# Attention, two mixtures of experts: another order for the last expert, narrower passes for two others

## The chip, the cores and the metric

One core of one Trainium2 chip runs the whole program. The metric is the device time of one execution in microseconds (us). Engines are named as in the profile: PE is TensorE (PEld its weight loads), ACT is ScalarE, DVE is VectorE, POOL is GpSimd, SP is SyncE, which issues most transfers.

## The reference

Three stages follow each other. The change touches the second and its seam to the third.

```python
# 1: attention over 4 x 8 heads, window 32 and 32 global tokens; x is [2176, 512]
# 2: top-1 mixture of 8 experts
logits = x @ w_gate
e_idx = np.argmax(logits, axis=1)
...
for e in range(E):                        # E = 8
    mask = e_idx == e
    h = np.maximum(x[mask] @ w1[e], 0.0)  # 512 -> 1024
    ye = h @ w2[e]                        # 1024 -> 512
    out[mask] = gate_w[mask, None] * eom[mask, e, None] * ye
# 3: the last stage, 512 -> 2048 -> 512, with a rational function between
h = x @ w_in
P = a[0] + a[1] * h + a[2] * h2 + a[3] * h3
Q = 1.0 + np.abs(b[0]) * np.abs(h) + np.abs(b[1]) * h2
g = P / (Q + 1e-06)
return g @ w_out
```

The inputs of the measurement send 422, 331, 253, 249, 220, 149, 434 and 118 tokens to the experts 0 to 7.

## The kernel before, in words

**Numbers.** Each float32 operand of these products is split into a rounded part (`fp32r`, "hi") and the rest ("lo"); a product is made of hi x hi, hi x lo and lo x hi. ScalarE makes the hi part with a cast, and VectorE or GpSimd the lo part with a subtraction. Weights come in 16 pieces of 128 x 512 an expert (`split_piece`); pieces 0 to 7 are w1, 8 to 15 are w2. There are two weight buffers, `slot[0]` and `slot[1]`, in turn, and four raw buffers, so that a raw load waits until the pieces two loads back are split.

**A wide pass** (`wide`, lines 918 to 960) holds weights in TensorE and streams an expert's tokens: in each of 8 steps 12 matmuls make 128 rows of h for n tokens (line 932), ScalarE and VectorE make ReLU with hi and lo (937, 938), and two steps later 12 matmuls add to four accumulators (944). That is 192 matmuls of n columns. `WIDE` gives n for some experts, `BASE` = 256 for the others. At the end four copies (950) bring the result to `yt`, and two DMAs on ScalarE's queue store it (952, 869).

**A single block** (`single`, 875 to 916) does it the other way round: 128 tokens lie in TensorE, and the weights stream past them, 512 columns a matmul. 24 matmuls make h with tokens in rows (895), a ReLU (898), 8 transposes (883) with casts and subtractions (809, 810) turn it, then products by w2 (905), two copies that make `y` (910 by ScalarE, 911 by VectorE), four transposes (914), a copy (915) and a store. With `parts=2` the second products have 256 columns and use two accumulators, with `parts=1` 512 and one. `beyond(e)` runs it behind a branch when an expert has more tokens than its pass; here that happens for expert 0 and for expert 6. It stands behind the first step of the next expert's pass.

**Side work.** While TensorE works through a pass, `todo` gives the other engines work at fixed points, *ticks*: `wide` takes one tick after every six matmuls. `plan` says what is done at which tick: "s" splits a weight piece of the next expert, "c" does one of three operations that convert a piece of w_in or w_out from its 64-bit form (`conv_step`, VectorE; 18 pieces, three at each of experts 1 to 6, with a load and a store by SP), "g" gathers 128 tokens, "x" scales and "p" transposes and splits them. In expert 7's pass (`PLANW7`) the pieces split are those of w_in for the last stage (`MODE7`: how), and `first_steps` is woven in: it splits the first 512 rows of stage 3's input into `x2c` (`x2_prep`, 1189 and 1190), and does the first two of the last stage's 16 groups: per group 12 matmuls in two halves ("m"), and in five parts ("e") the rational function: three activations, a GpSimd product and two VectorE operations; Ln and Exp; three VectorE operations; the rounding (1182); the subtraction (1184).

**The seam.** Behind expert 7 come `beyond(7)`, a first spare product of the last stage (group 2), the split of two W_out pieces (`first_w`, 1117 and 1118), a branch for rare inputs (1126) and a second spare product (group 3, both line 1150). Then the last stage runs in steps of 12 + 12 matmuls (1150 and 1295). All engines take their instructions in the order in which the program gives them.

Of the kernel before, what the change touches and what calls it, by code (L numbers as in the profile page):

```python
# [7 lines left out]
F32 = mybir.dt.float32  # L8
# [34 lines left out]
READY, WIDE = (6,), {0: 296, 1: 332, 6: 308}  # L43
# [13 lines left out]
NPRE, NCONV = 2, 9  # L57
# [3 lines left out]
PLANW = plan(32, s=range(0, 31, 2), c=(2, 3, 4, 12, 13, 14, 22, 23, 24), g=(1, 3, 18, 24), x=(1, 2, 14, 16), p=(5, 8, 19, 22))  # L61
PLANW7 = plan(30, s=(0, 5, 6, 8, 9, 11, 12, 14, 15, 17, 18, 20, 21, 23, 24, 25))
# [38 lines left out]
MODE7 = ("act",) + ("act_pool",) * 15  # L101


class Build:
# [731 lines left out]
    def experts(self, st, first, gate):  # L836
# [38 lines left out]
        def single(e, to, x, at=0, put=None, parts=2):  # L875
# [16 lines left out]
            for n in range(2):  # L892
                ph = ps_a.tile([128, 512], F32, tag=f"acc{n + 1}", name=f"acc{n + 1}")
                for i, (k, a, b) in enumerate(ORDER):
                    nc.tensor.matmul(ph, lhsT=x[:, a, k, at:at + 128], rhs=W[:, b, 2 * k + n, :], start=(i == 0), stop=(i == 11))
                    if i % 3 == 2:
                        hook(n, i // 3)
                nc.scalar.activation(hr[n], ph, AF.Relu)
            w = 512 // parts
            py = [ps_a.tile([128, 512], F32, tag=f"acc{m}", name=f"acc{m}")[:, 0:w] for m in (0, 3)[:parts]]  # L900
            for ks in [(k,) for k in range(6)] + [(6, 7)]:
# [5 lines left out]
                for k in ks:  # L907
                    hook(2, k)
            y, yc = hr[0], hr[1].rearrange("p (c t) -> p c t", c=4)
# [52 lines left out]
        def todo(e, plan, half=None, blocks=(), gathers=(), mode=SPLIT_MODE):  # L962
# [3 lines left out]
            k = NCONV * (e - 1)  # L966
# [26 lines left out]
        blocks = lambda e, bs=range(4): [(e, b, b) for b in bs if e < E]  # L993

# [29 lines left out]
        def expert(e, early=lambda: ()):  # L1024

            plan = PLANW if e < E - 1 else PLANW7
            more_ = blocks(e + 1, (2, 3)) if e + 1 in READY else [None] * 2
            wide(e, wd(e), X(e), weave(todo(e, plan, None, blocks(e + 1, (0, 1)) + more_, more_ + blocks(e + 2, (0, 1))),
# [65 lines left out]
        def first_steps(at=None):  # L1094

            def tick(n):
                while at and at[0] < n:
                    at[0] += 1
                    yield
            for n in range(CH[0]):  # L1100
                yield from tick(1 + n)
                self.x2_prep(n, self.x2c, n)
            h = [ps_t().tile([128, 4, 128], F32, tag="pt", name="pt").rearrange("p c t -> p (c t)") for _ in range(2)]
            gens = [self.first_elem(k, h[k], hr[k]) for k in range(2)]
            order = [("m", 0), ("m", 0), ("e", 0), ("m", 1), ("m", 1), ("e", 0), ("e", 1), ("e", 0), ("e", 1), ("e", 1)]
            parts = [self.product_parts(h[k], self.x2c, k, 512) for k in range(2)]
            for i, (c, k) in enumerate(order):
                yield from tick(8 + i + i // 2)
                next(parts[k] if c == "m" else gens[k], None)
            for k, t in enumerate(GT + (30, 30)):  # L1110
# [8 lines left out]

        expert(E - 2, early)  # L1120
        expert(E - 1, lambda: first_steps([0]))
# [348 lines left out]
```

## Time and profile before

| | us |
|---|---|
| median of 3 runs | 778.82 (778.63 to 778.91) |
| the profiled execution | 779.69 |
| its span, first to last instruction | 778.0 |
| busy in the span: PE / PEld | 757.1 / 652.5 |
| busy in the span: DVE / ACT / POOL | 584.4 / 527.3 / 352.7 |
| mean granted TensorE clock | 0.993 |

The profiled execution is one of its own, 0.11% above the median; stretches are read from its trace and set against its own time. A busy PE is not a PE at its peak, since matmuls overlap: for what a matmul costs, the distance from one start to the next is read.

### The profile page before, as it was taken

How to read it: one execution, taken by the hardware profiler on the slowest of the kernel's cores; microseconds unless marked ns; L12 is line 12 of the kernel's file. 1: busy time of each engine (PE TensorE's matmuls, PEld its weight loads, DVE VectorE, ACT ScalarE, POOL GpSimd, SP SyncE). 2: the span in 40 equal slices, each digit the busy share in tenths (PEclk: the TensorE clock that was granted, in tenths of full speed). 3: DMA queues.
4: the chain of work that ended last, by engine and by line, in shares of the span. 5: the costliest groups of instructions: out<-in, count | busy, mean ns of one | idle time of the engine just before them, and what ended most of it. 6: DMA issues, size and time to landing. Idle time of an engine off the chain costs nothing. (4 is left out here: it accounts for less than half of the span.)

```text
span 778.0 us, 16683 instructions
## 1 busy us (share of the span) xinstructions
PE 757.1 (97%) x5976; PEld 652.5 (84%) x5976; DVE 584.4 (75%) x1419; ACT 527.3 (68%) x1181; POOL 352.7 (45%) x439
## 2 busy tenths in 40 slices
PE   8998999899999999999999999999999999999996
PEld 5776776698999999998978888898888898989984
DVE  5777788683568877772389998888888768997983
ACT  4666775555455656643778887778777767887872
POOL 4445664523255556541756866532342214322422
PEclk9999999999999999999999999999999999999998
DMA  8998885555588999893463340110010000000101
GB/s 290 323 312 273 291 269 144 144 168 184 191 279 285 316 304 334 287 306 114 127 195 109 109 108 1 51 45 14 1 54 14 1 1 27 28 1 1 40 1 40
DMA packets 51978, 112.55 MB, mean 145 GB/s; under 512 B 10194, under 2 KB 24274, under 8 KB 49832
## 3 DMA queue, kind: packets, MB, share of 16 engines
q1 hardware_dynamic: 42232, 96.39, 39.1%
q0 software_dynamic: 3168, 9.27, 3.4%
q10 hardware_dynamic: 6480, 5.65, 2.3%
q8 instruction: 52, 0.85, 0.5%
q14 instruction: 46, 0.38, 0.2%
HBM read 93.58 MB, written 18.77 MB: 144 GB/s over the span
## 5 line engine op out<-in xcount | busy, mean ns | idle before, releaser
L1256 POOL TENSOR_TENSOR q<-q,ab 128x384 f32<-128x384 f32 (+1 forms) x78 | 93.9, 1204 | 212.1 <-ACT q L1255 205.1
L1295 PE MATMUL acc<-slot,gh 128*128 128x512 f32 x528 | 165.7, 394 | 0.0
L699 POOL TENSOR_TENSOR slot<-raw,slot 128x512 fp32r<-128x512 f32 x66 | 90.3, 1377 | 89.0 <-ACT slot L695 86.9
L1150 PE MATMUL ph<-x2c,slot 128*128 128x512 f32 (+1 forms) x552 | 125.1, 374 | 0.9 <-DVEq L1126 0.6
L1150 PEld LDWEIGHTS ph<-x2c,slot 128*128 128x128 f32 x552 | 101.1, 187 | 19.6 <-DVEq L1126 0.9
L1295 PEld LDWEIGHTS acc<-slot,gh 128*128 128x128 f32 x528 | 98.3, 187 | 20.1 <-ACT gh L1267 0.2
L944 PE MATMUL acc<-hT,slot 128*128 128x256 f32 (+3 forms) x768 | 109.2, 292 | 0.0
L1295 PE MATMUL acc<-slot,gl 128*128 128x512 f32 x264 | 104.4, 395 | 0.0
L944 PEld LDWEIGHTS acc<-hT,slot 128*128 128x128 f32 x768 | 101.9, 189 | 0.2
L695 ACT CAST slot<-raw 128x512 fp32r<-128x512 f32 x128 | 75.0, 618 | 7.6 <-DVE yt L950 4.0
L316 POOL TENSOR_SCALAR pr<-ex,r 128x128 f32<-128x128 f32 x128 | 47.0, 379 | 60.8 <-PE sc L263 21.0
L1150 PE MATMUL ph<-xa,slot 128*128 128x384 f32 x384 | 71.8, 336 | 0.0
L1150 PEld LDWEIGHTS ph<-xa,slot 128*128 128x128 f32 x384 | 67.9, 188 | 2.7
L1267 ACT CAST gh<-u 128x384 fp32r<-128x384 f32 (+1 forms) x78 | 43.3, 555 | 39.0 <-PE acc L1295 20.8
L699 DVE TENSOR_TENSOR slot<-raw,slot 128x512 fp32r<-128x512 f32 x62 | 55.0, 890 | 14.9 <-ACT slot L695 14.4
L1270 ACT ACTIVATE r<-q,cab 128x384 f32<-128x384 f32 (+1 forms) x78 | 51.3, 657 | 19.3 <-POOL q L1256 18.7
L937 ACT ACTIVATE hT<-ph 128x256 fp32r<-128x256 f32 (+3 forms) x64 | 25.7, 401 | 50.8 <-PE ph L932 40.1
L1295 PEld LDWEIGHTS acc<-slot,gl 128*128 128x128 f32 x264 | 49.4, 187 | 12.3 <-DVE gl L1268 0.3
L298 ACT ACTIVATE ex<-sm,mx 128x128 f32<-128x128 f32 x128 | 50.3, 395 | 13.9 <-POOL pr L316 7.0
L1255 ACT ACTIVATE q<-ab,cab 128x384 f32<-128x384 f32 (+1 forms) x78 | 58.3, 747 | 0.9
L1255 ACT ACTIVATE u<-ph,cab 128x384 f32<-128x384 f32 (+1 forms) x78 | 55.0, 705 | 4.0 <-POOL gl L1268 2.8
L932 PE MATMUL ph<-xa,slot 128*128 128x256 f32 (+1 forms) x384 | 54.6, 292 | 1.2 <-PEq L1040 0.4
(235 smaller groups left out, 1471.0 us busy)
## 6 DMA issues: line engine op xcount, KB each, us to landing
raw<-in_w_dram SPq DMA_DIRECT2D x78, 512.0 KB
vw<-in_vw_dram SPq DMA_DIRECT2D x16, 1024.0 KB
r<-in_w_dram SPq DMA_DIRECT2D x18, 512.0 KB
kw<-in_kw_dram SPq DMA_DIRECT2D x16, 384.0 KB
raw<-wf SPq DMA_DIRECT2D x9, 512.0 KB
qt<-in_qT_dram SPq DMA_DIRECT2D x32, 128.0 KB
xbuf<-xrow SPq DMA_DIRECT2D x8, 512.0 KB
xg<-ybuf SPq DMA_DIRECT2D x13, 256.0 KB
```

What stands on the lines that cost most here:

```text
L298: nc.scalar.activation(ex[:, h], src[:, h], AF.Exp, bias=mx[:, h:h + 1], scale=-1.0, accum_out=ssum[:, h:h + 1])
L316: nc.gpsimd.tensor_scalar(out=pr[:, h], in0=ex[:, h], scalar1=r[:, h:h + 1], scalar2=1.0, op0=ALU.mult, op1=ALU.mult)
L695: nc.scalar.copy(hi, r)
L699: eng.tensor_tensor(out=lo[:, c], in0=r[:, c], in1=hi[:, c].bitcast(F32), op=ALU.subtract)
L932: nc.tensor.matmul(ph, lhsT=W[:, b, 2 * k + s // 4, c:c + 128], rhs=x[:, a, k, :n], start=(i == 0), stop=(i == 11))
L944: nc.tensor.matmul(acc[m][:, :n], lhsT=W[:, b, 8 + f, 128 * m:128 * m + 128], rhs=hT(f % nh, n)[:, a], start=(f == 0 and i == 0), stop=(f ...
L1150: self.nc.tensor.matmul(ph[:, :w], lhsT=l[a], rhs=r[b], start=(k == 0 and i == 0), stop=(k == 3 and i == 2))
L1255: nc.scalar.activation(o_, x_, AF.Identity, scale=k1, bias=k0)
L1256: nc.gpsimd.tensor_tensor(out=q, in0=q, in1=ab, op=ALU.mult)
L1267: nc.scalar.copy(g[0], up)
L1270: nc.scalar.activation(r0, q, AF.Ln, bias=eps1)
L1295: nc.tensor.matmul(accs[i], lhsT=l[a], rhs=Wo[:, b, f, :], start=(f == 0 and j == 0), stop=(f == 15 and j == 2))
```

## The change

Expert 7 has no wide pass any more: behind expert 6's pass comes `beyond(6)`, then `single` for expert 7's 128 tokens with `parts=1`, and the side work and the last stage's first two groups are taken from inside it (`bg`): a tick after three matmuls of the first products, after each ReLU, and after each of the eight steps of the second, 16 in all; what is left of the side work follows behind `single`. `ORDER1` puts the parts of the two groups on ticks; their accumulators are now `acc3` and `acc1`, and a scratch tile is part of `yt`. `PLANW7` has 18 ticks, and in `MODE7` two pieces have their subtraction on VectorE instead of one. The result of expert 7 is stored by `put_last`. Experts 4 and 5 get passes of 224 and 160 columns. The 18 conversions go to the experts as `PIECES` says: 6, 3, 3, 2, 1, 3 for experts 1 to 6. Expert 7 has one block of tokens gathered and prepared, not two (`pair`).

```diff
--- before.py
+++ after.py
@@ -40,7 +40,7 @@
 NB = 2
 BASE, MOST, LAG = 256, 512, 2
 NX = 4
-READY, WIDE = (6,), {0: 296, 1: 332, 6: 308}
+READY, WIDE = (6,), {0: 296, 1: 332, 4: 224, 5: 160, 6: 308, 7: 128}
 FIRST = WIDE[0]
 SA, S0, S1 = "v", "a", "a"
 
@@ -54,12 +54,18 @@
     return o
 
 
-NPRE, NCONV = 2, 9
+NPRE = 2
+PIECES = 0, 6, 3, 3, 2, 1, 3, 0
 
 LOADS = [(f, f + 1) for f in range(0, NPRE, 2)] + [(f,) for f in range(NPRE, 16)]
 WLO = lambda nc, f: nc.vector if f < 3 else nc.gpsimd
-PLANW = plan(32, s=range(0, 31, 2), c=(2, 3, 4, 12, 13, 14, 22, 23, 24), g=(1, 3, 18, 24), x=(1, 2, 14, 16), p=(5, 8, 19, 22))
-PLANW7 = plan(30, s=(0, 5, 6, 8, 9, 11, 12, 14, 15, 17, 18, 20, 21, 23, 24, 25))
+EACH = {6: (1, 4, 8, 12, 16, 20), 3: (2, 12, 22), 2: (3, 12), 1: (12,), 0: ()}
+PLANW = lambda e: plan(32, s=range(0, 31, 2), c=[k + n for k in EACH[PIECES[e]] for n in range(3)], g=(1, 3, 18, 24), x=(1, 2, 14, 16), p=(5, 8, 19, 22))
+PLANW7 = plan(18, s=(0, 0, 5, 5, 6, 7, 9, 9, 11, 11, 12, 13, 14, 15, 16, 17))
+ORDER1 = ((4, "m", 0), (5, "m", 0), (8, "e", 0), (9, "m", 1), (11, "m", 1), (11, "e", 0), (13, "e", 1), (14, "e", 0),
+          (16, "e", 1), (17, "e", 1))
+GT1 = 18, 19
+ORDER0 = tuple((0, c, int(k)) for c, k in ("m0", "m0", "e0", "m1", "m1", "e0", "e1", "e0", "e1", "e1"))
 EY = 11, 1, 11, 1
 GT = 25, 27
 ORDER = 13
@@ -98,7 +104,7 @@
 W0 = lambda s: s >= 25
 NWARM = 12
 SPLIT_MODE = ("act_pool", "act")
-MODE7 = ("act",) + ("act_pool",) * 15
+MODE7 = ("act",) * 2 + ("act_pool",) * 14
 
 
 class Build:
@@ -872,7 +878,7 @@
 
             nc.sync.dma_start(out=self.ybuf[:, :, FIRST:FIRST + 128], in_=y)
 
-        def single(e, to, x, at=0, put=None, parts=2):
+        def single(e, to, x, at=0, put=None, parts=2, bg=iter(())):
 
             W = self.slot[e % 2]
             hk = lambda a, k: hT(AFTER + k // 2, BASE)[:, a, 128 * (k % 2):128 * (k % 2) + 128]
@@ -895,7 +901,10 @@
                     nc.tensor.matmul(ph, lhsT=x[:, a, k, at:at + 128], rhs=W[:, b, 2 * k + n, :], start=(i == 0), stop=(i == 11))
                     if i % 3 == 2:
                         hook(n, i // 3)
+                        if i < 11:
+                            next(bg, None)
                 nc.scalar.activation(hr[n], ph, AF.Relu)
+                next(bg, None)
             w = 512 // parts
             py = [ps_a.tile([128, 512], F32, tag=f"acc{m}", name=f"acc{m}")[:, 0:w] for m in (0, 3)[:parts]]
             for ks in [(k,) for k in range(6)] + [(6, 7)]:
@@ -906,6 +915,7 @@
                                              start=(k == 0 and i == 0), stop=(k == 7 and i == 2))
                 for k in ks:
                     hook(2, k)
+                    next(bg, None)
             y, yc = hr[0], hr[1].rearrange("p (c t) -> p c t", c=4)
             nc.scalar.copy(y[:, :256], py[0][:, 0:256])
             nc.vector.tensor_copy(y[:, 256:], py[-1][:, w - 256:w])
@@ -963,7 +973,7 @@
 
 
             sp = self.split_set(e + 1, mode if e < E - 1 else MODE7, half)
-            k = NCONV * (e - 1)
+            k = 3 * sum(PIECES[:e])
             gs, xs, ps, ns = iter(gathers), iter(blocks), iter(blocks), self.counts()
             for do in plan:
                 for c in do:
@@ -992,6 +1002,8 @@
 
         blocks = lambda e, bs=range(4): [(e, b, b) for b in bs if e < E]
 
+        pair = lambda e: blocks(e, range(min(2, -(-wd(e) // 128)))) + [None] * (wd(e) <= 128)
+
         def fetch(e, i):
 
             ixo = self.ixo[:, 0:1]
@@ -1023,9 +1035,9 @@
 
         def expert(e, early=lambda: ()):
 
-            plan = PLANW if e < E - 1 else PLANW7
+            plan = PLANW(e) if e < E - 1 else PLANW7
             more_ = blocks(e + 1, (2, 3)) if e + 1 in READY else [None] * 2
-            wide(e, wd(e), X(e), weave(todo(e, plan, None, blocks(e + 1, (0, 1)) + more_, more_ + blocks(e + 2, (0, 1))),
+            wide(e, wd(e), X(e), weave(todo(e, plan, None, pair(e + 1) + more_, more_ + pair(e + 2)),
                                          iter(early())), before=(lambda: beyond(e - 1)) if e > 1 else second)
 
         def beyond(e):
@@ -1093,21 +1105,28 @@
 
         def first_steps(at=None):
 
+            order, late = (ORDER1, GT1) if at else (ORDER0, (0, 0))
+
             def tick(n):
                 while at and at[0] < n:
                     at[0] += 1
                     yield
             for n in range(CH[0]):
-                yield from tick(1 + n)
+                yield from tick(n)
                 self.x2_prep(n, self.x2c, n)
-            h = [ps_t().tile([128, 4, 128], F32, tag="pt", name="pt").rearrange("p c t -> p (c t)") for _ in range(2)]
-            gens = [self.first_elem(k, h[k], hr[k]) for k in range(2)]
-            order = [("m", 0), ("m", 0), ("e", 0), ("m", 1), ("m", 1), ("e", 0), ("e", 1), ("e", 0), ("e", 1), ("e", 1)]
-            parts = [self.product_parts(h[k], self.x2c, k, 512) for k in range(2)]
-            for i, (c, k) in enumerate(order):
-                yield from tick(8 + i + i // 2)
-                next(parts[k] if c == "m" else gens[k], None)
-            for k, t in enumerate(GT + (30, 30)):
+            h, parts, gens = {}, {}, {}
+            for t, c, k in order:
+                yield from tick(t)
+                if c == "m":
+                    if k not in h:
+                        acc = f"acc{3 - 2 * k}"
+                        h[k] = ps_a.tile([128, 512], F32, tag=acc, name=acc)
+                        parts[k] = self.product_parts(h[k], self.x2c, k, 512)
+                        gens[k] = self.first_elem(k, h[k], yt.rearrange("p m t -> p (m t)")[:, 512 * k:512 * k + 512])
+                    next(parts[k], None)
+                else:
+                    next(gens[k], None)
+            for k, t in enumerate(late + late):
                 yield from tick(t)
                 next(gens[k % 2], None)
 
@@ -1117,8 +1136,18 @@
                 nc.scalar.copy(hi, w)
                 nc.vector.tensor_tensor(out=lo, in0=w, in1=hi.bitcast(F32), op=ALU.subtract)
 
+        def put_last(y):
+            k = 128 - NBLK * (E - 1)
+            YQ(nc).dma_start(out=self.toks[bass.ds(off[E - 1], 128 * k), :].rearrange("(j p) o -> j (p o)", p=128),
+                             in_=self.idxT[NBLK * (E - 1):])
+            store(E - 1, 0, 128, y, YQ(nc))
+
         expert(E - 2, early)
-        expert(E - 1, lambda: first_steps([0]))
+        beyond(E - 2)
+        side = weave(todo(E - 1, PLANW7), first_steps([0]))
+        single(E - 1, 0, X(E - 1), parts=1, bg=side, put=lambda y: put_last(y))
+        for _ in side:
+            pass
         beyond(E - 1)
         self.bank = [ps_h.tile([128, 512], F32, tag="ph", name="ph") for _ in range(PRE)]
         first_w()
```

## Rows read from the trace of the kernel before

**Rows 1.** Windows, experts 1, 5, 7: PE, PEld, DVE, ACT, POOL busy; clock, DMA, GB/s.

```profile
184.00:226.00 42.00, 40.95 (x268) 39.20 (x269) 21.03 (x31) 17.69 (x36) 12.96 (x11) 1.00 0.61 198
298.30:323.45 25.15, 25.00 (x211) 24.83 (x210) 20.25 (x32) 16.68 (x35) 16.83 (x12) 1.00 0.96 330
367.20:394.70 27.50, 27.40 (x204) 26.08 (x204) 13.02 (x24) 21.27 (x42) 20.86 (x17) 1.00 0.39 126
```

**Rows 2.** Timeline of TensorE, 350 to 404 us: start, us, what [idle before <-releaser].

```profile
351.98 1.60 PE L932 MATMUL ph<-xa,slot 128*128 128x256 f32 x12
353.42 4.25 PE L895 MATMUL acc<-slot,x2c 128*128 128x512 f32 x18
357.51 0.60 PE L883 MATMUL pt<-ident,hr 128*128 128x128 f32 x4
357.86 1.65 PE L895 MATMUL acc<-slot,x2c 128*128 128x512 f32 x6
...
367.24 3.14 PE L932 MATMUL ph<-xa,slot 128*128 128x256 f32 x24 [0.43 <-PEq L1040]
...
394.79 3.64 PE L1150 MATMUL ph<-x2c,slot 128*128 128x512 f32 x13
399.03 2.83 PE L1150 MATMUL ph<-x2c,slot 128*128 128x512 f32 x11 [0.59 <-DVEq L1126]
401.70 2.68 PE L1295 MATMUL acc<-slot,xa 128*128 128x512 f32 x11
```

**Rows 3.** Timeline of ScalarE, 358 to 398 us.

```profile
358.14 0.37 ACT L809 CAST hT<-pt 128x256 fp32r<-128x256 f32 x1 [1.20 <-PE pt L883]
359.01 0.37 ACT L809 CAST hT<-pt 128x256 fp32r<-128x256 f32 x1 [0.49 <-DVE hT L810]
...
367.82 0.62 ACT L695 CAST slot<-raw 128x512 fp32r<-128x512 f32 x1 [0.34 <-ACTq L1040]
...
377.58 0.60 ACT L1166 ACTIVATE hr<-pt 128x512 f32<-128x512 f32 x1 [2.30 <-issue]
...
379.44 0.38 ACT L937 ACTIVATE hT<-ph 128x256 fp32r<-128x256 f32 x1
379.71 1.66 ACT L695 CAST slot<-raw 128x512 fp32r<-128x512 f32 x3
...
394.51 0.31 ACTq L952 DMA_DIRECT2D toks<-idxT  x1
...
396.27 1.14 ACT L1117 CAST slot<-raw 128x512 fp32r<-128x512 f32 x2 [1.58 <-ACTq L1037]
```

**Rows 4.** Timeline of VectorE, 386 to 391 us.

```profile
388.11 0.68 DVE L1176 SCALAR_TENSOR_TENSOR xg<-xg,pt 128x512 f32<-128x512 f32 x1
```

**Rows 5.** Weight loads by shape, whole span: busy us, mean ns | idle before.

```profile
L944 PEld LDWEIGHTS acc<-hT,slot 128*128 128x128 f32 x768 | 101.9, 189 | 0.2
...
L883 PEld LDWEIGHTS pt<-ident,hr 128*128 128x128 f32 x16 | 1.9, 140 | 0.3
...
L339 PEld LDWEIGHTS pt<-ident,exg 128*32 128x32 f32 x8 | 0.8, 98 | 0.0
```

**Rows 6.** Windows around the one fall of the clock behind the start.

```profile
135.70:139.13 3.43, 2.29 (x33) 1.32 (x29) 2.08 (x11) 2.03 (x7) 3.36 (x7) 1.00 0.62 158
139.13:142.54 3.41, 3.36 (x30) 2.32 (x34) 2.01 (x9) 1.86 (x7) 2.99 (x6) 0.50 0.01 2
```

**Rows 7.** Timeline of TensorE in the passes of experts 4 and 5.

```profile
291.31 1.59 PE L944 MATMUL acc<-hT,slot 128*128 128x256 f32 x12
292.74 1.54 PE L932 MATMUL ph<-x2c,slot 128*128 128x256 f32 x12
294.12 1.10 PE L944 MATMUL acc<-hT,slot 128*128 128x256 f32 x8
...
311.16 1.60 PE L932 MATMUL ph<-xa,slot 128*128 128x256 f32 x12
312.59 0.64 PE L944 MATMUL acc<-hT,slot 128*128 128x256 f32 x4
```

## The prediction

> **What bounds the kernel now.** I read the windows first, one per stage. In the pass of expert 5 TensorE is busy 25.00 of 25.15 us, ScalarE 16.68, VectorE 20.25; in the rest of expert 7's pass TensorE is busy 27.40 of 27.50, ScalarE 21.27, GpSimd 20.86 [rows 1]. So TensorE sets the time of both stretches, but in the second the other engines are not far behind. Then the timeline of TensorE from expert 6's last product to the third product of the last stage, to see where it waits: 0.43 us behind the single block of expert 6, and 0.59 us ahead of the second spare product, released by VectorE passing a branch [rows 2]. Then the timelines of ScalarE and VectorE in the same stretch, for the price and the order of what has to fit beside TensorE [rows 3, 4]. Last, weight loads by shape and a fall of the clock [rows 5, 6].
>
> **Expert 4 at 224 and expert 5 at 160 columns.** Each pass keeps its 192 matmuls; only the columns shrink. Today 12 matmuls of 256 columns take 1.38 us in expert 4's first product (292.74 to 294.12) and 1.43 in its second (291.31 to 292.74), 1.43 in expert 5 (311.16 to 312.59) [rows 7]: 115, 119 and 119 ns each. If time went with columns, 224 would take 102 and 160 would take 74 ns. Against that stand the weight loads. A load is recorded with 98 ns for 32 columns and 140 for 128 in the plain transposes, so 84 ns are fixed and 0.44 ns go to each column; the loads of the expert products are recorded with 189 ns, which leaves 105 for their 128 columns [rows 5]. As one load follows each matmul and one matmul each load, I estimate a floor of 105 to 114 ns, 110 taken: at 256 columns the matmul hides the load, below it the load is what is seen. Expert 4: 96 x 5 + 96 x 9 ns = 1.3 us; expert 5: 192 x 9.5 ns = 1.8 us. Bounds: 0.5 us for both if loads take 117 as these passes do now at their slowest end, 11 if columns counted in full.
> The Trainium skill's page "TensorE: Matmul & The Clock Gate", section "Back-to-back issue gap", gives 81 ns a matmul at 128 columns and 131 at 512 with loads included; an estimate between these is 85 ns at 160 and 93 at 224, and 11 us from both passes. The rows here have 18 matmuls of 512 columns in 4.09 us, 227 ns each [rows 2], so its figures do not hold for this kernel's number format, and I keep 110.
> What else these passes do shrinks too (ReLU, stores). Conversions move from experts 4 and 5 to expert 1: costed at nothing, since VectorE was busy 21.03 of 42.00 us there and the DMA share was 0.61, against 0.96 in expert 5 [rows 1]; nine more operations of about 0.7 us fit. Without that cover they would cost about 6 us.
> Expert 7 gathers one block, not two: four transposes less, 357.51 to 357.86 [rows 2], 0.35 us of TensorE.
>
> **Expert 7 on TensorE.** Removed: a pass of 192 matmuls. It runs today from 351.98, stands aside from 353.42 to 367.24 for expert 6's single block (which stays as it is), and ends at 394.79, with 24 matmuls of the last stage inside [rows 2]: 1.44 + 27.55 = 29.0 us. Added: 48 matmuls of 512 columns, 8 transposes and the same 24: 72 x 0.233 + 0.7 = 17.5 us (0.233 is 2.8 us for twelve in the last stage; the single block shows 0.227). On TensorE alone 11.5 us fall away. But the cover for the rest goes with them.
>
> **Expert 7 on ScalarE.** I count from t = 0, the first matmul of expert 7 behind the single block (367.24 in the trace). ScalarE then starts at 0.6 (367.82) [rows 3]. Its work in order, casts at 0.52 (three in 1.66 us): pieces 0 and 1, three x2c casts, a ReLU, the fourth x2c cast: to 4.2. VectorE's subtractions behind them (0.6 each) end at 5.0. The first group's first product now stands at tick 4, 15 matmuls in (3.5); it needs all four x2c blocks and so waits to 5.1, 1.4 us of TensorE. All behind it slides: the four transposes start at 7.0, and their casts, next in ScalarE's queue, at 7.6. ScalarE idles 3.4 us, since pieces 2 onwards are queued behind them. Then: two transposed casts with a subtraction between (358.14 to 359.01, 1.2 with the second), pieces 2 to 5 (2.1), a ReLU (0.5), the first three activations of group 0 (377.58 to 379.44: 1.86), pieces 6 and 7, two casts (1.2), pieces 8 and 9, Ln and Exp (1.3), 10 and 11, three activations of group 1 (1.86), 12 and 13: the copy of y starts at 21.7. TensorE's own work was over at 18.9.
> Half of y is VectorE's. Its queue has group 1's two operations, which wait for ScalarE (to 21.5), then group 0's last three (0.7 each, 388.11 onwards [rows 4]), then the copy: 23.6 to 24.0. The last transposes end at 24.3: TensorE has waited 5.4 us (3.2 and 1.9, two transposes between). The new edit hangs TensorE's queue on a copy behind 13 casts; in the old pass the output copies held nothing up.
> Next late is the second spare product. It waits for VectorE past the branch at line 1126, as today (399.03, with 0.59 us idle), and VectorE comes there behind the two W_out pieces. ScalarE from 25.2: two DMA issues (394.51 to 396.27 today with the branch behind them, 1.4 taken; they are put before pieces 14 and 15), piece 14, Ln and Exp, piece 15, one group's rounding: 29.5; the other's waits for VectorE's three operations to 30.9; then the W_out casts (1.1) to 32.8, VectorE's subtraction to 33.7. The spare product resumes at 33.7 and the first second product of the last stage starts at 36.3. Today: 399.03 and 401.70, which is 31.8 and 34.5 behind 367.24; with the 1.44 us that no longer run ahead of the single block, 35.9. So this stretch comes out at +0.4 us: ScalarE's queue is the new bound, and TensorE's 11.5 us turn into waits (1.4 + 5.1 + 6.6, less 1.3 that it waits today). GpSimd is not late: 14 subtractions and two products at 1.25 (17 instructions in 20.86 [rows 1]) end near 30.5. Raw loads come in time, each issued four pieces ahead. My bounds for the whole queue, from a start or a wait misjudged at each of its three waits: -2.5 to +2.5.
>
> **The clock.** From 135.70 to 139.13 TensorE was busy 2.29 of 3.43 us, and the next 3.41 us ran at a granted 0.50, 1.2 GHz; then 1.00 again [rows 6]. TensorE would now idle 6.6 us ahead of the second spare product. One such stretch costs half of itself, 1.7 us, if TensorE has work all through. I take +1.6, between 0 (the stretch falls in the wait) and 3.4 (two stretches). The skill's same page, section "What's actually happening", states that the low clock is the default and activity lifts it; the rows show one fall, and by that rule one more here gives the same 1.7.
>
> **Sum**: -1.3 - 1.8 - 0.35 + 0.4 + 1.6 = -1.4 us. The profiled execution took 779.69 us (span 778.0), 0.9 above the median 778.82; so 778.3 for it and **777.4** for the median. Behind this stretch nothing gives it back: TensorE runs without a gap there, and what the stretch loses or gains stays.
>
> **Rivals.**
> - *ScalarE's queue is shorter than I lay it* (27%). Its work up to the W_out casts is 24.4 us, so without the three waits the spare product would resume near 26; half of that distance is 4 us, and with y ready by 20.5 the clock does not fall: -3.45 - 3.6 = -7, 771.8. For it: the queue is near its work sum today too. Against: the waits follow from queue order.
> - *Columns count below 256* (6%): 11 us from experts 4 and 5 in place of 3.1, 769.5. For it: 115 to 119 ns at 256 and 227 at 512 are nearly in proportion. Against: the recorded load of 189 ns. The page's spacing above would bring the same result.
> - *Slower: the low clock covers both spare products* (17%). If TensorE falls during the wait for y, the first spare product takes twice its 2.8 us and the fall is renewed in the longer wait; both products and the start of the next run at 1.2 GHz, +3.4 in place of 1.6, and the rounding of group 2 follows late by some 2 us: 781.2. It decides from where clock and queue together cost over 3.45 us, the sum of the sure gains. Against: nothing in rows 6 lasts over one stretch.
> - *Narrow passes are dearer than 256* (4%): the trace has no such matmul under 256 columns. From 119 to 128 ns a matmul would take back expert 4's and 5's gain and as much again: 782.
>
> **Chances.** My forecast has 46%, with a range of its own of 775 to 780.5: 21 points lie more than 0.2% (1.6 us, about what a measurement of this kernel can tell from no change) below 778.82, 21 within and 4 above. Faster 0.21 + 0.27 + 0.06 = 0.54; same 0.21 + 0.02 of the third rival = 0.23; slower 0.04 + 0.15 + 0.04 = 0.23. The range of 8 in 10 goes down to 770, which takes in the first rival and leaves out the second, and up to 782, past the third.
>
> **What would show it.** Expert 4 and 5: twelve matmuls in 1.30 to 1.35 us whatever the columns. Expert 7: an idle TensorE ahead of the last four transposes, released by a VectorE copy, some 5 us; ScalarE with no gap there; a second wait of 6 us, released by VectorE past the branch for rare inputs; a granted clock of 0.50 in that wait. Wrong if ScalarE reaches y before TensorE is done, if twelve matmuls of 160 columns take 0.9 us, or if the clock stays at 1.00.

## The result, and the profile after

The kernel became slower: 782.22 us, median of 19 runs, against 778.36 us for the kernel before in 19 runs beside it; the ratio is 1.0062, with a 95% interval of 1.0048 to 1.0075. The forecast was 777.4 us. The profiled execution after has a span of 784.9 us, 6.9 more than the one before, and a mean clock of 0.980. It is not a typical one: with 786.55 us it was the slowest of the 19 and had the lowest clock (median 0.986), so the stages read from it below add up to more than the 3.9 us between the medians. A few executions of five of the later kernels, up to three of twelve, took some 20 us more at a lower clock, and the times below leave them out.

The first look is at the length of each stage, from the start of its first matmul to the start of its last, worked out from the timelines of TensorE of both kernels, in us. "E7 stretch" is the time from there, the start of expert 6's last matmul, to the first second product of the last stage (401.70 in the kernel before [rows 2], 408.22 after).

```
                   before    after    difference
expert 1            45.03    50.26      +5.23
expert 2            23.63    24.85      +1.22
expert 3            24.13    24.13       0
expert 4            23.57    22.57      -1.00
expert 5            24.98    23.30      -1.68
expert 6            28.31    27.89      -0.42
E7 stretch          49.86    52.71      +2.85
                                        +6.20
```

Three rows lose, and the forecast spoke of the last of them alone. Expert 1's pass now holds six pieces' conversions in place of three. Its windows, and those of its last part (columns as in [rows 1]; the first answers to the first row there, and lies 1.8 us later in the pass):

```profile
186.00:228.00 42.00, 39.20 (x258) 37.10 (x256) 21.21 (x36) 17.13 (x34) 12.96 (x10) 1.00 0.67 225
226.00:232.00 6.00, 2.62 (x9) 2.63 (x10) 4.38 (x7) 0.72 (x2) 0.68 (x1) 0.68 0.83 273
224.00:228.10 4.10, 1.82 (x12) 1.55 (x11) 2.62 (x3) 0.05 (x1) 2.52 (x3) 1.00 1.01 385
228.10:234.95 6.85, 5.57 (x22) 5.40 (x22) 3.49 (x7) 1.49 (x3) 0.00 (x0) 0.50 0.85 287
```

VectorE is busy for half of the 42 us, as before (21.21 us, 21.03 before), so it is not full, but TensorE is busy for only 2.62 of the 6 us at the end, and then runs for 6.85 us at a granted 0.50. The list of waits of the same pass (engine, line, waited for; us in total, times, longest) says why:

```profile
DVE f L737 <- DMA wf<-f: 4.3, 1, 4.3
...
DVE f L737 <- DMA r<-in_w_dram: 3.7, 2, 2.4
PE acc L954 <- DVE hT L948: 3.6, 1, 3.6
```

And the timeline of VectorE, cut to the conversions' first operation (L737) and the queue behind the last wait:

```profile
209.40 0.43 DVE L737 TENSOR_SCALAR f<-r 128x512 int32<-128x512 int32 x1 [1.29 <-DMA r<-in_w_dram]
...
216.92 0.43 DVE L737 TENSOR_SCALAR f<-r 128x512 int32<-128x512 int32 x1 [4.28 <-DMA wf<-f]
...
225.45 1.53 DVE L737 TENSOR_SCALAR f<-r 128x512 int32<-128x512 int32 x1 [2.40 <-DMA r<-in_w_dram]
227.01 0.69 DVE L740 SCALAR_TENSOR_TENSOR f<-r,f 128x512 int32<-128x512 int32 x1
227.62 0.68 DVE L705 TENSOR_TENSOR slot<-raw,slot 128x512 fp32r<-128x512 f32 x1
228.22 0.69 DVE L743 SCALAR_TENSOR_TENSOR f<-r,f 128x512 int32<-128x512 int32 x1
228.82 0.50 DVE L948 SCALAR_TENSOR_TENSOR hT<-ph,hT 128x332 fp32r<-128x332 f32 x1
```

TensorE in the same place:

```profile
221.69 4.13 PE L954 MATMUL acc<-hT,slot 128*128 128x332 f32 x26
229.38 3.14 PE L954 MATMUL acc<-hT,slot 128*128 128x332 f32 x10 [3.56 <-DVE hT L948]
```

The last of these operations had what it needs since ScalarE's row

```profile
221.89 0.45 ACT L947 ACTIVATE hT<-ph 128x332 fp32r<-128x332 f32 x1 [2.46 <-PE ph L942]
```

Together these rows show a chain. The first operation of a piece waits for the piece's own load (`r`), or for the store of the piece that used the same scratch tile (`f`): pieces 2 and 3 both take `f32[0]`, as `q % 3 % 2` is 0 for both. VectorE takes its queue in order, so the subtraction L948, whose operands were there from 222.34 on, stands until 228.82 behind a conversion that waits for a transfer, and TensorE waits for L948. Of the pass's 5.23 us that wait is 3.56; most of the rest is the low clock behind it, which also covers the start of expert 2's pass. The Trainium skill's page "Perfetto Trace Analysis", section "Tensor Engine Instruction (MATMUL, LD_WEIGHTS)", states that VectorE's execution queue is strictly first in, first out; the trace agrees, with L948 begun only 0.60 us behind the start of L743, 6.48 us after its operands were there.

The last expert, on TensorE (answers to [rows 2]; the block's first matmul is at 369.96):

```profile
369.96 3.72 PE L901 MATMUL acc<-slot,xa 128*128 128x512 f32 x15 [0.78 <-ACTq L1052]
374.25 0.50 PE L1179 MATMUL acc<-x2c,slot 128*128 128x512 f32 x1 [0.56 <-ACT x2c L1218]
...
392.11 0.69 PE L924 MATMUL pt<-ident,hr 128*128 128x128 f32 x2 [2.98 <-ACT hr L920]
394.06 0.69 PE L924 MATMUL pt<-ident,hr 128*128 128x128 f32 x2 [1.26 <-DVE hr L921]
...
394.90 4.81 PE L1179 MATMUL ph<-x2c,slot 128*128 128x512 f32 x12
402.42 6.00 PE L1179 MATMUL ph<-x2c,slot 128*128 128x512 f32 x12 [2.71 <-ACTq L1155]
408.22 3.30 PE L1324 MATMUL acc<-slot,xa 128*128 128x512 f32 x12
```

and the windows of the clock there:

```profile
388.50:391.97 3.47, 0.63 (x3) 0.19 (x1) 1.84 (x3) 3.47 (x7) 3.47 (x4) 1.00 0.47 163
391.97:398.80 6.83, 5.28 (x13) 3.72 (x14) 2.61 (x5) 3.27 (x7) 6.28 (x6) 0.50 0.66 205
402.20:409.03 6.83, 6.47 (x14) 4.75 (x15) 4.70 (x8) 3.98 (x8) 1.29 (x1) 0.50 0.48 157
```

The waits are where the forecast put them, but the clock falls twice and each time for 6.83 us, so both spare products run at 1.2 GHz for most of their time: the first takes 4.81 us (3.04 at full clock, in e6_warm below), the second 5.80 from its start to the start of what follows (3.10 there).

The two narrower passes (answers to [rows 7]), expert 4 and then expert 5:

```profile
292.15 1.50 PE L954 MATMUL acc<-hT,slot 128*128 128x224 f32 x12
293.49 1.51 PE L942 MATMUL ph<-x2c,slot 128*128 128x224 f32 x12
...
314.73 1.50 PE L954 MATMUL acc<-hT,slot 128*128 128x160 f32 x12
316.07 1.50 PE L942 MATMUL ph<-xa,slot 128*128 128x160 f32 x12
```

Twelve matmuls take 1.34 us from start to start, at 224 columns and at 160.

### The profile page after: what moved, and what is told of

It is laid out like the page before. It is cut to its first block, busy times and chain, and to the rows that moved or that the text cites. A ratio compares the mean times of both kernels' runs of the same rounds, so it can differ in the third digit from the quotient of the medians.

```text
span 784.9 us, 16389 instructions
## 1 busy us (share of the span) xinstructions
PE 752.8 (96%) x5840; PEld 642.2 (82%) x5840; DVE 579.9 (74%) x1414; ACT 523.0 (67%) x1177; POOL 348.2 (44%) x437
## 5 line engine op out<-in xcount | busy, mean ns | idle before, releaser
L705 POOL TENSOR_TENSOR slot<-raw,slot 128x512 fp32r<-128x512 f32 x65 | 88.4, 1367 | 99.6 <-ACT slot L701 97.4
L1179 PE MATMUL ph<-x2c,slot 128*128 128x512 f32 (+1 forms) x552 | 129.4, 383 | 3.0 <-ACTq L1155 2.7
L1179 PEld LDWEIGHTS ph<-x2c,slot 128*128 128x128 f32 x552 | 104.0, 193 | 23.0 <-ACTq L1155 3.1
L954 PE MATMUL acc<-hT,slot 128*128 128x256 f32 (+5 forms) x672 | 96.2, 294 | 3.6 <-DVE hT L948 3.6
L954 PEld LDWEIGHTS acc<-hT,slot 128*128 128x128 f32 x672 | 89.7, 192 | 3.8 <-DVE hT L948 3.8
L947 ACT ACTIVATE hT<-ph 128x256 fp32r<-128x256 f32 (+5 forms) x56 | 21.7, 388 | 48.6 <-PE ph L942 40.3
L1289 DVE SCALAR_TENSOR_TENSOR u<-u,cab,ph 128x384 f32<-128x384 f32 (+1 forms) x78 | 51.9, 666 | 2.8
```

Of the source, the lines that this page charges most:

```text
L705: eng.tensor_tensor(out=lo[:, c], in0=r[:, c], in1=hi[:, c].bitcast(F32), op=ALU.subtract)
L954: nc.tensor.matmul(acc[m][:, :n], lhsT=W[:, b, 8 + f, 128 * m:128 * m + 128], rhs=hT(f % nh, n)[:, a], start=(f == 0 and i == 0), stop=(f ...
L1179: self.nc.tensor.matmul(ph[:, :w], lhsT=l[a], rhs=r[b], start=(k == 0 and i == 0), stop=(k == 3 and i == 2))
L1289: nc.vector.scalar_tensor_tensor(out=u, in0=u, scalar=a1, in1=h, op0=ALU.add, op1=ALU.mult)
```

## The experiments

Theory W, formed from these rows: the loss is the conversions' new place, through their transfers. Rival B: it is the last expert's block. Rival L, below: it is the nine more operations themselves. The first four runs split the change into its parts. All times are medians of 6 to 12 runs; ratios, with their intervals, are to the kernel before, run beside them (778.3 us in the first two groups, 779.1 and 778.7 in the last ones). A difference taken from medians and one taken from ratios can part by some 1.6 us.

**e1_even: the change with the conversions left where they were.**

```diff
-PIECES = 0, 6, 3, 3, 2, 1, 3, 0
+PIECES = 0, 3, 3, 3, 3, 3, 3, 0
```

> The changed kernel with the 18 conversions back at three for each of experts 1 to 6; all else as changed. Theory W (the six conversions in expert 1 make VectorE wait for their own transfers, and TensorE falls idle and cold behind it): expert 1's pass back from 50.3 to about 45.0 us, expert 2's from 24.85 to 23.6, the granted clock at 1.00 there; 6.4 us less than the changed kernel in the profile, about 778 us, within 0.2% of the kernel before. Theory B (the loss is the last expert's block, and expert 1's stall is an accident of one profiled execution): under 2 us less than the changed kernel, still about 0.4% above the kernel before.

Measured: 778.78 us, ratio 0.9998 (0.9980 to 1.0015). Expert 1's pass is 44.97 us again and expert 2's 23.72; no conversion waits for a transfer. One line of numbers carries the whole difference between the change and no change. Its size is less sure than its sign: 3.4 us by the medians, 5.0 by the ratios.

**e2_pieces: the kernel before with that line alone.**

```diff
-k = NCONV * (e - 1)
+k = 3 * sum(PIECES[:e])     # PIECES = 0, 6, 3, 3, 2, 1, 3, 0
```

> The kernel before with the conversions alone moved (6, 3, 3, 2, 1, 3 for experts 1 to 6). Theory W: slower by 4 to 6.4 us (about 783 us), expert 1's pass near 50 us, with VectorE waiting there for a store and two loads of the conversions, 8 us in all. Theory B: within 0.2% of the kernel before.

Measured: 784.37 us, ratio 1.0085 (1.0055 to 1.0115): 6.1 us by the medians, the largest effect of any part. Its waits in expert 1 are the same as those of the whole change, somewhat longer:

```profile
DVE f L733 <- DMA wf<-f: 5.0, 1, 5.0
...
DVE f L733 <- DMA r<-in_w_dram: 4.1, 2, 2.9
...
PE acc L946 <- DVE hT L940: 3.6, 1, 3.6
```

**e3_widths: the kernel before with 224 and 160 columns for experts 4 and 5.**

```diff
-{0: 296, 1: 332, 6: 308}
+{0: 296, 1: 332, 4: 224, 5: 160, 6: 308}
```

> The kernel before with expert 4 at 224 and expert 5 at 160 columns, nothing else. Both passes at 112 to 113 ns a matmul, whatever the columns: 1.0 and 1.7 us less in these passes, 2.7 us in all (775.6 us, 0.35% faster). A rival: three conversions in the shortened passes make them wait, and less than 1.5 us is left.

Measured: 776.11 us, ratio 0.9970 (0.9949 to 0.9990). Expert 4's pass falls to 22.57 and expert 5's to 23.68 us: 2.3 us in both together, 0.4 less than expected, all of it in expert 5.

**e4_block: the change with even conversions and without the narrower passes**, so that the last expert's block and its schedule are left.

```diff
-PIECES = 0, 6, 3, 3, 2, 1, 3, 0
+PIECES = 0, 3, 3, 3, 3, 3, 3, 0
-WIDE = (6,), {0: 296, 1: 332, 4: 224, 5: 160, 6: 308, 7: 128}
+WIDE = (6,), {0: 296, 1: 332, 6: 308, 7: 128}
```

> The kernel before with the last expert's block and its side work alone: three conversions for each expert, experts 4 and 5 at 256 columns. From the changed kernel's trace: the stretch from expert 6's last product to the last stage's first second product 2.9 us longer than before, less 0.4 us of saved transposes: 2.4 us slower (780.8 us, 0.3%). The other theory (the block itself gives the 11.5 us of TensorE back, and only the conversions lose): faster by 0.4% or more.

Measured: 781.17 us, ratio 1.0027 (1.0010 to 1.0044). The block loses 2 to 3 us by itself. The three ratios multiply to 1.0027 x 0.9970 x 1.0085 = 1.0082, somewhat above the 1.0062 of the whole, within what their intervals allow. Rival B falls as the main cause: block and widths cancel (e1_even), and the conversions decide.

The next runs ask what it is in the conversions, and what it is in the block.

**e5_buffers: six conversions in expert 1, with the scratch tile changed for pieces 3 to 5.**

```diff
-self.conv_op(self.r64[q % 2], self.f32[q % 3 % 2], n)
+f = self.f32[q % 2 if q < 6 else q % 3 % 2]
+self.conv_op(self.r64[q % 2], f, n)
```

> The changed kernel with six conversions still in expert 1, but the fourth piece goes to the other scratch buffer, so that it does not wait for the third piece's store to land. Theory W (VectorE stands in its queue behind the conversions' transfers, and TensorE behind VectorE): the wait of 4.28 us for the store is gone, part of it comes back as a wait for the fourth piece's own load, which was hidden behind it (up to 2.4 us, as the other two); expert 1's pass falls from 50.26 us to 46 to 48, no low clock in expert 2, and the kernel is 2 to 4 us faster than the changed one: 778.5 to 780.5 us. Rival L (nine more VectorE operations of 0.7 us are 6 us of work, whatever they wait for): pass of expert 1 above 49.5, time 781 to 782.5 us.

Measured: 783.54 us, ratio 1.0062 (1.0037 to 1.0088): no gain. The wait for the store of piece 2 is gone as expected, and expert 1's pass falls to 48.83 us, but expert 2's rises to 26.38, and the sum of both stays (75.21 against 75.11). The edit moved piece 5 into the other tile, which is a part of `yt`, where the pass ends by copying its output. The list of waits, 205 to 236 us:

```profile
DVE yt L961 <- DMA wf<-yt: 3.7, 1, 3.7
...
ACT yt L961 <- DMA wf<-yt: 9.7, 1, 9.7
```

Now the output copies wait for the store of piece 5. The forecast of W missed, and the run does not tell W from L.

**e9_spread: six conversions, evenly spaced, tiles strictly by turns, the last one not in `yt`.**

```diff
-EACH = {6: (1, 4, 8, 12, 16, 20), ...
+EACH = {6: (2, 7, 12, 17, 22, 27), ...
+f = self.f32[(q + 1) % 2 if q < 6 else q % 3 % 2]
```

> The changed kernel with six conversions in expert 1, spread evenly over its pass (every fifth place, from the third to the 30th of 32) and with the two scratch buffers strictly by turns, the last piece in the one that the end of the pass does not write. A piece's load then has ten places from its issue to its use, some 14 us, in place of six to eight, and no piece waits for the store of the one before. Theory W1 (it is the short notice of each transfer that stalls VectorE): the conversions' waits fall below 2 us in total, expert 1's pass takes 45 to 47 us, the kernel 778.5 to 780 us. Theory W2 (the bytes themselves are late: three more pieces are 3 x 768 KB, about 6 us at the 380 to 400 GB/s that the end of this pass moves): waits of 4 us and more stay in expert 1 or move into expert 2, 781 to 783 us. Rival L (the nine operations on VectorE): pass above 49.5 us with few waits, 782 us.

Measured: 780.03 us, ratio 1.0013 (0.9995 to 1.0032). The conversions' waits for transfers fall from 8.0 us to 0.5, and expert 1's pass takes 45.01 us with all six pieces in it: it was the short notice of the transfers, of loads or stores, since spacing and tiles were changed together. The time is just above W1's 780 us because expert 2's pass takes 27.27 us. On TensorE:

```profile
222.41 1.53 PE L943 MATMUL ph<-x2c,slot 128*128 128x256 f32 x12
224.09 1.65 PE L943 MATMUL ph<-x2c,slot 128*128 128x256 f32 x12
227.51 2.73 PE L943 MATMUL ph<-x2c,slot 128*128 128x256 f32 x12 [1.76 <-DVEq L1050]
```

VectorE has the last piece's operations ahead of its copies of the pass's output, arrives 1.76 us late at the branch, and the clock follows (0.50 from 227.77 for 3.41 us). So with this order the last place in the pass costs again, though hardly by a wait for a transfer (0.54 us).

**e10_repeat: eighteen operations in expert 1, but three pieces' transfers.** Each piece's three operations run twice on the same data; the first time without store and load.

```diff
+if twice:
+    q, again = divmod(q, 2)
+    if not again:
+        return self.conv_op(self.r64[q % 2], self.f32[q % 3 % 2], n)
```

> e1_even with eighteen conversion operations in expert 1 at the places of the changed kernel, but for three pieces only: each piece's three operations run twice on the same data, and its store and the next load are issued once, after the second time. So VectorE has the nine more operations without one more byte of transfers. Theory W: expert 1's pass 45 to 46.5 us, VectorE's waits for transfers no longer than in e1_even, the kernel within 1.5 us of e1_even's 778.8. Rival L (the nine operations themselves): pass near 50 us, 782 us and more.

Measured: 778.98 us, ratio 1.0009 (0.9986 to 1.0032). Expert 1's pass takes 45.05 us, with VectorE busy 26.14 us in this window of 43 us:

```profile
183.00:226.00 43.00, 41.52 (x273) 39.49 (x272) 26.14 (x41) 17.90 (x36) 13.41 (x12) 1.00 0.60 193
```

In the same window of e1_even's pass it is 21.50 us:

```profile
184.00:227.00 43.00, 41.58 (x272) 39.58 (x272) 21.50 (x33) 17.70 (x36) 13.84 (x12) 1.00 0.61 199
```

Nine more operations cost nothing here. Rival L falls, and W stands: the operations were free, their transfers were not.

**e6_warm: e1_even with matmuls that nobody reads in TensorE's two waits**, twelve ahead of the transposes of y and six ahead of the branch.

```diff
+fill(12)      # ahead of y's transposes
...
 self.first_product(0)
+fill(6)
 with tc.If(rare[0] > 0):
```

> The changed kernel with three conversions in each expert (e1_even), and with matmuls whose product nobody reads in TensorE's two waits at the end of the last expert's block: twelve ahead of the transposes of y (2.8 us), six between the two spare products (1.4 us). They add no wait of their own as far as they fit into waits of 4.5 and 2.2 us. If the low clock costs what the rows of e1_even say (spare products of 5.46 and 4.75 us in place of 2.8): the granted clock stays 1.00, both products take 2.8 to 3.0 us; the first one's gain disappears in the wait for ScalarE's queue at the branch behind it, the second one's is kept: 1.5 to 2.5 us faster than e1_even, 776.3 to 777.3 us. Rival (the last stage is bound by the elementwise chain, and the second spare product is needed only there): within 0.5 us of e1_even's 778.8.

Measured: 776.22 us, ratio 0.9976 (0.9951 to 1.0000); 2.6 us below e1_even by the medians, 1.7 by the ratios, whose intervals overlap, so that the gain rests on the trace. There the clock is 1.00 from 385 to 405 us, and the E7 stretch is 49.98 us, 1.61 less than in e1_even:

```profile
387.85 3.04 PE L1187 MATMUL ph<-x2c,slot 128*128 128x512 f32 x12
393.77 1.66 PE L884 MATMUL acc<-slot 128*128 128x512 f32 x6 [2.89 <-ACTq L1056]
395.59 3.27 PE L1187 MATMUL ph<-x2c,slot 128*128 128x512 f32 x12
```

The six stand behind the second wait, not in it; the clock held all the same. They delay next to nothing, since the spare product's second matmul (396.02) stands behind VectorE's last subtraction ahead of the branch, which ends at 395.91. Without low clock the stretch is 0.12 us longer than in the kernel before (49.86): that is what the block costs with its waits alone.

**e7_seam: e1_even with both spare products ahead of the branch.**

```diff
 self.first_product(0)
+self.first_product(1)
 with tc.If(rare[0] > 0):
     ...
     self.first_product(0)
-self.first_product(1)
+    self.first_product(1)
```

> e1_even with the second spare product issued ahead of the branch for rare inputs (the branch's body, which never runs here, redoes both). TensorE's wait of 2.2 us for ScalarE's queue at the branch then lies behind both products: the second ends about 399 in place of 402.7, and the last stage's first second product starts there. Theory Q (ScalarE's queue up to the branch, then TensorE's spare product, set the start of the last stage): 2 to 4 us faster than e1_even, 775 to 777 us. Rival (the elementwise chain bounds, it starts at the branch in both): within 0.7 us of 778.8.

Measured: 774.7 us, ratio 0.9953 (0.9927 to 0.9978), 4.1 us below e1_even by the medians, 3.5 by the ratios: theory Q.

```profile
385.63 8.36 PE L1180 MATMUL ph<-x2c,slot 128*128 128x512 f32 x24
394.29 3.00 PE L1325 MATMUL acc<-slot,xa 128*128 128x512 f32 x12 [0.30 <-PEq L1156]
```

Both products still run at a low clock (8.36 us for 24), but within the time that TensorE would have waited at the branch; the E7 stretch is 48.00 us in place of 51.59. The last stage takes some of it back: from its first second product to the end it is 378.0 us, 376.5 in e1_even.

**e8_late: e1_even with y's copies ahead of the work that stood before them.**

```diff
-    next(bg, None)
+    if k < 6:
+        next(bg, None)
-(13, "e", 1), (14, "e", 0)
+(14, "e", 0), (15, "e", 1)
```

> e1_even with y's two copies ahead of the last two pieces of Wi, of group 0's last three VectorE operations and of group 1's first part, all of which follow behind y. TensorE's wait before the transposes of y falls from 4.5 us (2.97 and 1.51) to about 1. Theory Q: TensorE then waits at the branch instead, since ScalarE has the same work to do; only ScalarE's own wait for the transposes (2.73 us in e1_even) gets shorter, and the chain of group 1 starts 3 us later: 0 to 1.5 us faster than e1_even, 777.3 to 778.8 us. Rival Y (y's wait itself is on the path): 3 to 4 us faster, 775 to 776 us.

Measured: 777.96 us, ratio 0.9987 (0.9955 to 1.0019).

```profile
382.99 0.90 PE L925 MATMUL pt<-ident,hr 128*128 128x128 f32 x4 [0.46 <-ACT hr L921]
384.04 3.04 PE L1180 MATMUL ph<-x2c,slot 128*128 128x512 f32 x12
396.05 0.79 PE L1180 MATMUL ph<-x2c,slot 128*128 128x512 f32 x1 [8.97 <-ACTq L1156]
```

The wait for y falls from 4.48 to 0.46 us, and the time moves by 0.8, which the intervals do not tell from nothing: the same ScalarE queue is waited for 8.97 us at the branch. The E7 stretch is no shorter, 52.83 us in place of 51.59, and with that rival Y falls.

**e11_best: e7_seam with a shorter queue on ScalarE.**

```diff
-nc.scalar.copy(yc, pt)
+(nc.vector.tensor_copy if put and e == E - 1 else nc.scalar.copy)(yc, pt)
-store(E - 1, 0, 128, y, YQ(nc))
+store(E - 1, 0, 128, y, nc.sync)
+fill(12)      # ahead of y's transposes; the tokens' store goes to nc.sync, too
```

> e7_seam (even conversions, the second spare product ahead of the branch) with ScalarE's queue shortened at the end of the last expert's block: VectorE in place of ScalarE copies the transposed y (0.6 us, and ScalarE's wait of 2.73 us for the transposes goes), y's store and its tokens' are issued by SyncE's queue; and twelve matmuls that nobody reads keep TensorE busy ahead of the transposes of y. Theory Q (ScalarE's queue up to the branch sets the start of the last stage): the branch 3 to 4 us sooner, both spare products at full clock (5.7 us in place of 8.36), 2 to 3.5 us faster than e7_seam: 771.3 to 772.8 us. Rival (the elementwise chain of group 1 on VectorE and GpSimd bounds, ScalarE only waits for it): within 1 us of 774.75.

Measured: 774.8 us, ratio 0.9955 (0.9938 to 0.9972): no gain over e7_seam, the rival's outcome. Both spare products run at full clock and the E7 stretch falls to 46.75 us, but the last stage then takes 379.3 us in place of 378.0. The branch is now released by VectorE, and ScalarE behind it waits for the store that was moved:

```profile
396.71 0.60 ACT L1290 ACTIVATE ab<-ph 128x512 f32<-128x512 f32 x1 [3.37 <-DMA ybuf<-hr]
```

**e12_best2: the store back on ScalarE's queue, four of GpSimd's subtractions to VectorE.**

```diff
-MODE7 = ("act",) * 2 + ("act_pool",) * 14
+MODE7 = ("act",) * 2 + ("act_pool",) * 6 + ("act",) * 4 + ("act_pool",) * 4
```

> e11_best with y's store back on ScalarE's queue (in e11_best the last stage's first elementwise operation waited 3.37 us for that store), and with four of Wi's second halves (pieces 8 to 11) subtracted by VectorE in place of GpSimd, whose multiplication for group 1 stood 2.4 us behind them. If, with ScalarE's queue shortened, the chain of group 1 over GpSimd and VectorE is what the branch waits for, the branch comes 2 to 3 us sooner than in e7_seam, and the time is 771.5 to 773.5 us. If the branch is no longer what starts the last stage (its elementwise chain runs 378.1 us from its first operation to the end in both e7_seam and e11_best, whenever that starts), or VectorE's four more operations delay y: within 1 us of e7_seam's 774.75.

Measured: 773.7 us, ratio 0.9931 (0.9908 to 0.9955), the lowest of all, but not told apart from e7_seam (0.9927 to 0.9978). The expected 2 to 3 us did not come: issuing the store now waits in ScalarE's queue for VectorE's copy.

```profile
392.33 0.62 ACT L701 CAST slot<-raw 128x512 fp32r<-128x512 f32 x1 [4.16 <-DVE hr L932]
```

## Why the prediction was wrong, step by step

- **Conversions moved to expert 1, "costed at nothing": this is the step that failed.** It measured +5.23 us in expert 1 and +1.22 in expert 2 of the profiled execution; alone, 6.1 us (e2_pieces). The cover that the step named was VectorE's idle half and the DMA share of 0.61. The first is real: nine more operations cost nothing there (e10_repeat). The second was the wrong thing to read. A mean share over 42 us does not say whether one piece's load or store lands in the few us until the next piece needs its tile; in the last 4.1 us before the clock fell the share was 1.01. With six pieces close together in two tiles they did not land, and in VectorE's queue the subtraction that TensorE needs stands behind. The "about 6 us" that the step gave for lost cover came out near the measurement, but for another reason: it priced operations, and the loss is waits with the low clock behind them.
- **Expert 4 and 5 narrower: right in the price of a matmul, 0.4 us too large in the sum.** Forecast were -1.3 and -1.8 us, from a floor of 110 ns set by the weight loads; -1.00 and -1.68 were measured, with 1.34 us for twelve, 112 ns a matmul at either width. The forecast interval for twelve was 1.30 to 1.35. The Trainium skill's page "TensorE: Matmul & The Clock Gate", section "Back-to-back issue gap", gives 81 ns at 128 columns; the 112 ns at 160 here do not agree, and the measurement decides.
- **Four transposes less: right**, -0.35 forecast, -0.42 measured in expert 6's pass.
- **Expert 7 on ScalarE: right in its places and nearly in its sum.** Counted from the block's first matmul (369.96), y's copy on ScalarE was laid at 21.7 and came at 21.73 (391.69), VectorE's half at 23.6 and came at 23.63, the second spare product at 33.7 and came at 32.46, released by ScalarE, with its other eleven matmuls from 33.40 on, behind VectorE. TensorE's wait for y was 4.24 us, not 5.1, and the second 2.71, not 6.6: the first product, at the low clock, ended 2.65 us later than laid, and ScalarE came 1.24 us sooner. With the clock held up the stretch is 0.12 us longer than before (e6_warm); the forecast was +0.4. e8_late shows the reason given, too: shorten the wait for y, and ScalarE's queue is waited for later.
- **The clock: right in kind, too small.** It was taken as one stretch of 3.4 us, +1.6, because [rows 6] show one of that length. Here it fell twice, for 6.83 us each, and the second spare product took 5.80 us to the start of what follows, in place of 3.10 (e6_warm). The stretch less e6_warm's, 52.71 - 49.98, is 2.7 us. That is the third rival's mechanism, at 17%, with most of its price of 3.4. Other executions with the same block and seam have less of it: the stretch is 51.59 us in e1_even, 51.73 in e5_buffers, 52.12 in e4_block, 52.59 in e10_repeat and 52.66 in e9_spread, 1.61 to 2.68 above e6_warm's.
- **The first, second and fourth rivals did not come**: ScalarE reached y when forecast, columns below 256 do not count, and narrower matmuls are not dearer.

Put together: -1.00 - 1.68 - 0.42 + 2.85 is -0.25 us, the whole change without the conversions, and e1_even's ratio is 0.9998. That the two meet is partly luck: in e1_even's profile expert 5 gains only 0.56 us and the stretch loses only 1.73. The conversions add 6.45 in this profile; between e1_even and the change it is 3.4 us by the medians and 5.0 by the ratios. Against the forecast's -1.45 for these terms, -0.25 is 1.2 us dearer: the clock 1.1 too small, the widths' gain 0.4 too large, ScalarE's queue 0.3 too dear. The rest of the miss, and its sign, is the conversions. At 782.22 us the time lies just beyond the upper end of the range, 782.

Two things are left that the profiles settle in part. Expert 5's pass took 23.68 to 24.79 us in kernels that do the same work in it, with three conversions each. ScalarE waits there for gathered tokens, 2.7 us in e12_best2 (a pass of 23.68), 3.9 in e1_even (24.42) and 4.3 in e11_best (24.79); in the last two TensorE then waits for ScalarE ahead of four transposes, 0.54 and 0.91 us. In the changed kernel, with one conversion in that pass, ScalarE's wait is 1.2 us and TensorE has none (23.30). So some of the narrow pass's gain hangs on how late the gather lands, and why that differs stays open.

The other is what bounds the last stage. From its first second product to the end, 376.3 to 376.7 us pass in every profile but those of e7_seam, e11_best and e12_best2, which need 377.3 to 379.3. In these three the time from the first elementwise operation of the stage to the end is the same, 378.1 us (394.17 to 772.3 in e7_seam, 396.71 to 774.8 in e11_best); in the others it is 379.4 to 382.3. This points to TensorE as the bound where its second products start late, and to the elementwise chain in the three fastest kernels. A kernel that starts that chain sooner was not run.

## What to carry to other kernels

When work is moved into another stage's slack, give its transfers a schedule of their own: for each piece, from the issue of its load to its first use, and from its store to the next writer of the tile. An operation that waits for a transfer should not stand in an in-order queue ahead of one that the bounding engine needs; idle time of that engine and a mean DMA share don't show it.

And the branches of this kernel are meetings of engines: at the branch for rare inputs TensorE waited for VectorE before (0.59 us, [rows 2]) and for ScalarE after (2.71 us). Work of the bounding engine that may go ahead of such a branch should, because the wait is then covered (some 4 us here, between e1_even and e7_seam).

## What the runs showed of the hardware

A granted clock of 0.50 lasted 3.41 us in the kernel before [rows 6], but 6.83 us at three places after. The stretch in [rows 6] is not the only one behind the start of the kernel before: a second, from 70.86 to 74.27 us, lasted 3.41 us, too. In e1_even's and e5_buffers' profiles both lengths stand in the seam, 6.83 us at the first fall and 3.41 at the second. When it fell, TensorE stood in a wait, 2.3, 2.8 and 2.5 us after that wait had begun (225.8 to 228.10, 389.1 to 391.97, 399.7 to 402.20); and it rose again while TensorE was at work at the low clock.

Matmuls of 160 and 224 columns cost the same 112 ns, those of 256 115 to 119 [rows 7].

A profile's total hides small effects: nothing was changed ahead of expert 0's remaining pass, yet its first matmul came at 146.35 us in e9_spread's profile and at 153.30 in e12_best2's. From e9_spread's timeline of TensorE:

```profile
146.35 1.08 PE L943 MATMUL ph<-xs,slot 128*128 128x296 f32 x6 [0.49 <-ACT lgs L469]
```

and from e12_best2's:

```profile
153.30 1.09 PE L949 MATMUL ph<-xs,slot 128*128 128x296 f32 x6 [0.49 <-ACT lgs L469]
```

Totals could therefore be compared only over many runs. Between single profiles a stage could be compared to 0.1 us where TensorE never waits in it (expert 3's pass took 24.11 to 24.13 us in all fourteen), but not where a wait or the clock enters, as in expert 5's pass.
